# Three value blocks of the last pass turned ahead of wo's products: a decode step of two layers, forward and backward, on one core

## The chip, the core and the metric

The kernel runs on one core of a Trainium2 chip. The core has a matrix engine (TensorE: PE, with its weight loads PEld), a vector engine (VectorE: DVE), a scalar engine (ScalarE: ACT), a general engine (GpSimd: POOL), a queue engine (SyncE: SP) that here only issues transfers, and 16 DMA engines that move data between HBM and the on-chip memory SBUF. PE writes its results into PSUM, a small memory of eight banks, from where DVE or ACT fetch them. The metric is the device time of one execution in microseconds (us).

## The reference

Two attention layers and two MLP layers are interleaved and share their weights: A (attention with a key and a value cache of 16,384 positions, 2 sequences, 4 key/value heads, 32 query heads of 128), B (MLP), A, B. The kernel computes the output and the gradients of everything, the caches and the weights among them.

```python
def _A_ref(x, k_cache, v_cache, wq, wo):
    ...
    scores = jnp.einsum("bhqd,bhkd->bhqk", q, k) * (Dh ** -0.5)
    p = _softmax(scores, axis=-1)
    o = jnp.einsum("bhqk,bhkd->bhqd", p, v)
    return (lambda x, *d: x.transpose(*d))(o, 0, 2, 1, 3).reshape(B, Sq, Hq * Dh) @ wo
...
x = x + _A_ref(_layernorm(x, axis=-1), A_k_cache, A_v_cache, A_wq, A_wo)
x = x + _B_ref(_layernorm(x, axis=-1), B_w1, B_b1, B_w2, B_b2)
x = x + _A_ref(_layernorm(x, axis=-1), A_k_cache, A_v_cache, A_wq, A_wo)
x = x + _B_ref(_layernorm(x, axis=-1), B_w1, B_b1, B_w2, B_b2)
...
_out, _vjp = jax.vjp(_f, A_x, A_k_cache, A_v_cache, A_wq, A_wo, B_w1, B_b1, B_w2, B_b2)
_grads = _vjp(grad_out)
```

The last thing that the backward pass does is the attention backward of layer 0, the "last pass" here (`attn_bwd` with `l == 0`). For each of the 8 pairs of sequence and key/value head it needs the gradient's query vectors dO (the gradient that came down, times the transpose of wo), their products with all values V (the gradient of the probabilities), from these and the kept exponentials the gradient of the scores dS, and the products of dS with all keys (the gradient of the queries). In the same stretch the kernel writes the gradients of both caches (for both layers at once) and most weight gradients.

## The kernel before

**Passes.** The caches do not fit into SBUF, so every attention pass reads both from HBM once: forward layer 0, forward layer 1, backward layer 1, backward layer 0. A load brings 1 MB, 32 positions for each of the 128 partitions: a *chunk*, four *blocks* of 8 positions. Chunks go into slots (`slot0` to `slot15` and a few larger tiles that are free for a time).

**The order of the work.** All work is recorded first, as small functions with the slots that they use (`emit`), and replayed in that order (`Program.run`). The order on each engine is therefore the order of the recording; an engine that waits holds up everything behind it on the same engine. Loads are issued by SP in the order of their first use, each as early as a slot is free; SP's queue is in order too. A slot is free when the last recorded user of its chunk has run.

**A value block** (`kblock`). First a *turn* (L554): DVE transposes the block's 128x512 words in 32x32 squares into one of three `kT` buffers. Then a *use* (L567): eight PE products of the turned block with the spread query vectors `qbd`, into the PSUM bank `sc`. A use is recorded when two further turns have been recorded (`SKEW`), or at a step without a value block.

**The steps of the last pass.** `attn_bwd` runs steps 0 to 133. Step s turns value block s and multiplies key block s - 14 (L592); the last blocks are packed closer. In between stand the outputs: the dV and dK units (L1277, after a turn of the kept exponentials L1258 that ACT or DVE copies to `late`, L1265 or L1268), the weight gradients (L1337), and the spreading of q and dO over the partitions that these need (a transposition on PE L1225, a copy on ACT L1227 into `r16`, products L1235). Each output product fills a PSUM bank of 128x512; three banks take turns, and a cast by ACT (L276) or DVE (L279) empties each into a slot, from which POOL issues the store. Which of the two casts is fixed while recording, by a running account of both engines' load (`cast_out`, `copy_bf`, `load_of`).

**What stands ahead of step 0.** The gradient of layer 0's attention output is finished (L693, DVE: `gA_all`), wo's first 1024 rows, turned earlier, are multiplied with it (L470, 64 products, `here_products`), and `do_of` makes dO: L1018 and L1019 on DVE (`dof`, `qd`), four products L580 and two multiplications L583 that spread it into `qbd`, then the sums `dl` (L1022, a PE product L611, L1024). Three weight-gradient units of w2 (L1337) stand before L693 and one between wo's products; two more (`first[13:15]`) stand behind `do_of`. Then DVE clears an accumulator (L1057), and step 0 begins with the turn of value block 0. In step 4 `va` is spread (L511 on PE, L512 on DVE).

`wo_first` carries the recorded products of wo to `attn_bwd`; for layer 0 it is `(va0, wo_prods0)`. In these lines of step s the value blocks are recorded; `between` holds outputs and key blocks:

```python
for v in v_at.get(s, ()):
    pos, i = divmod(v, 16)
    if i % 4 == 0:
        kc[0] = ld_kv("V", order[pos], i // 4)
    kblock(kc[0], i, scb[0], order[pos], between)
```

Of the kernel before, what the change touches and what calls it, by code (L numbers as in the profile page):

```python
# [57 lines left out]
class Program:  # L58
# [12 lines left out]
    def emit(self, fn, uses=()):  # L71
        i = len(self.ops)
        self.ops.append((fn, tuple(uses)))
        for c in uses:
            if c.first is None:
                c.first = i
            c.last = i
# [105 lines left out]
def kernel(  # L183
# [25 lines left out]
    V = nc.vector  # L209
# [4 lines left out]
    B, _, D = A_x.shape  # L214
    _, HKV, SK, DH = A_k_cache.shape
# [14 lines left out]
    emit = P.emit  # L230
# [13 lines left out]
    scb = [[psp.tile([128, 8, 64], F32, name=f"sc{i}{f}") for f in range(2)] for i in range(2)]  # L244
# [37 lines left out]
    def dve(us):  # L282
        load_of("dve", us)
# [53 lines left out]
    def q_at(g):  # L337
        return 2 * (g % HKV % 2) + g // HKV
# [25 lines left out]
    saved = {}  # L364
# [11 lines left out]
    def ld_kv(nm, g, c):  # L376
        src = Kv if nm == "K" else Vv
        return P.chunk(lambda ap: nc.sync.dma_start(
            ap.rearrange("p (t d) -> p t d", d=128), src[g, :, c * 32:(c + 1) * 32, :]), (nm, g, c))
# [23 lines left out]
    pend = []  # L403
# [80 lines left out]
    def turned_products(ps, t, w0, nw, vb, first, last, parts=1):  # L484

        def f(k):
            def fn():
                tv = t.ap[:, 0:nw * 256].rearrange("p (w x e) -> p w x e", x=128, e=2)
                for w in range(k * nw // parts, (k + 1) * nw // parts):
                    for e in range(2):  # L490
                        J = (w0 + w) // 2
                        PE.matmul(ps(), lhsT=tv[:, w, :, e], rhs=vb()[:, 2 * (w % 2) + e, :, 2 * J:2 * J + 2],
                                  start=(first and w == 0 and e == 0), stop=(last and w == nw - 1 and e == 1),
                                  skip_group_check=True)
            return fn

        return [(f(k), [t]) for k in range(parts)]
# [47 lines left out]
            PE.matmul(ps[32 * a:32 * a + 32], lhsT=quadT[:], rhs=qa[:, :, a], start=True, stop=True)  # L545
        return ps.rearrange("p c (j b) -> p (c j) b", b=2)

    def kblock(c, i, bank, g, mids=()):

        hold = {}  # L550

        def turn():
            kT = ktp.tile([128, 1024], BF16, name="kT")
            V.transpose(out=kT[:].bitcast(I32).rearrange("p (w j m) -> p w j m", w=4, j=4),  # L554
                        in_=c.ap[:, (i % 4) * 1024:(i % 4 + 1) * 1024].bitcast(I32).rearrange(
                            "p (j w m) -> p w j m", w=4, j=4))
            dve(0.6)
            hold["kT"] = kT

        def use():  # L560
            kv = hold["kT"][:].rearrange("p (w m e) -> p w m e", w=4, e=2)
            sc = bank[i // 8].rearrange("p h (a y) -> p a h y", y=8)
            a0 = 4 * ((i // 4) % 2)
            for q in range(2):
                for w in range(2):
                    for e in range(2):
                        PE.matmul(sc[:, a0:a0 + 4, :, 2 * (i % 4) + q], lhsT=kv[:, 2 * q + w, :, e],  # L567
                                  rhs=qbd[:, q_at(g), 2 * w + e], start=(w == 0 and e == 0), stop=(w == 1 and e == 1))

        emit(turn, [c])  # L570
        for fn, us in mids:
            emit(fn, us)
        pend.append((use, ()))
        while len(pend) > SKEW:
            emit(*pend.pop(0))

# [413 lines left out]
    def wo_first_ops(l, k, ws=None):  # L990

        ws = ld_wo(k) if ws is None else ws
        ps = sb[0][:, 64:80].rearrange("p (r b) -> p r b", b=2)
        turns = [turn_here(ws[r // 4], (r % 4) * 1024, 8) for r in range(R)]
        prods = [here_products(ws[r // 4], (r % 4) * 1024, 8, lambda r=r: ps[:, r, :],
                               lambda o: gA_all[:, o, 2 * l:2 * l + 2]) for r in range(R)]
        return ws, turns, prods + [(lambda: do_of(l, k, ps), ())]
# [50 lines left out]
    def attn_bwd(l, order, gT, wo_first, outputs=None, mark=None, extra=None):  # L1048

        kvs = []  # L1050
        for g in order:
            if g % HKV not in kvs:
                kvs.append(g % HKV)
        vba, ops0 = wo_first
        for op in ops0:
            emit(*op)
        emit(lambda: V.memset(sb[0][:, 0:128], 0.0))  # L1057
        ev, wb = {}, {}
# [33 lines left out]
        for pos, g in enumerate(order):  # L1092
            quick = l == 0 and pos == G - 1
# [33 lines left out]
                for n, b in enumerate(ops):  # L1127
                    wb.setdefault((126 if l == 1 else 121) + n, []).append(b)

        kc, vc = {}, {}  # L1130
        n_steps = 128 + LAG_B if l == 1 else N_END
        k_at, v_at = {}, {}
        for v in range(128):
            quick = l == 0 and v >= 112
            k_at.setdefault(126 + v % 16 // 2 if quick else v + LAG_B, []).append(v)
            v_at.setdefault(112 + v % 16 // 2 if quick else v, []).append(v)
        s = 0
        while s <= n_steps:
            if s in (10, 74) and mark is not None:
# [3 lines left out]
            mids = []  # L1143
            for v in k_at.get(s, ()):
# [4 lines left out]
                c = vc[0]  # L1149
# [9 lines left out]
# [5 lines that stand above are left out]
                between = []  # L1164
# [130 lines left out]
    def y_rows(colT, j0, jn, q, at_):  # L1295

        def f():
            tp = ob().bitcast(BF16)[32 * q:32 * q + 4, 0:jn * 128].rearrange("p (a b) -> p a b", b=128)
            for j in range(jn):
                PE.transpose(tp[:, j, :], colT[:, j0 + j, :], ident[:])  # L1300
            S.copy(out=Y.ap[32 * q:32 * q + 4, at_:at_ + jn * 128], in_=flat(tp))
            load_of("act", 0.7)

        return f, [Y]
# [105 lines left out]
    up = [b * HKV + k for k in range(HKV) for b in range(2)]  # L1410
    down = up[::-1]
    marks = {}

    def mark(name):
        def f(n=0):
            marks[name, n] = len(P.ops)
        return f
# [61 lines left out]
    ws_o, wo_turns1, wo_prods = wo_first_ops(1, up[0] % HKV)  # L1479
# [28 lines left out]
    extra = {2: [(lambda: V.memset(fps1, 0.0), ())]}  # L1508
# [15 lines left out]
    for n, c in enumerate(ws1c):  # L1524
        t = w1t[n // 4][n % 4] if n == 7 else P.chunk()
        t1 += [] if n == 7 else turn_rows(c, t, 896)
        p1 += turned_products(lambda n=n: dm_0[:, n // 4], t, 14 * (n % 4), 14, vh0, n % 4 == 0, n % 4 == 3)
    attn_bwd(1, up, lambda: saved["g3"], (None, wo_prods), mark=mark("d1"), extra=extra)
    wo_prods0 = wo_first_ops(0, down[0] % HKV, saved["wo"])[2]


# [18 lines left out]
    first = [y_rows(gM_all, 0, 8, 0, 0)] + dw_units("h", 0, 0, pieces_rows(out_8, F, D))  # L1550
# [7 lines left out]
    va0, spread_a0 = spread(lambda: gA_all[:, :, 0:2], DJ, "va")  # L1558
# [3 lines left out]
    for u in first[9:12]:  # L1562
        emit(*u)
    emit(lambda: saved.__setitem__("g1", g1p[1]()))
    wo_prods0 = wo_prods0[:-1] + first[12:13] + wo_prods0[-1:] + first[13:15]
    extra = {4: [(spread_a0, ())]}

    sched = {}
# [20 lines left out]
    def outputs(s, rest=False):  # L1589
# [15 lines left out]
        state["credit"] = min(state["credit"], 2.0)  # L1605
        return res

    attn_bwd(0, down, lambda: saved["g1"], (va0, wo_prods0), outputs=outputs, extra=extra)
    slots = []
    for i, t in enumerate(slot_tiles):  # L1610
        until = marks[(HALF_AT + FULL_AT)[i], 0] if i < N_HALF + N_FULL else None
# [45 lines left out]
```

## Time and profile before

| what | value |
| --- | --- |
| three runs | 1099.14, 1101.32, 1103.54 us; median 1101.32 us |
| the profiled execution | 1099.65 us, of which 1097.9 us are the span from the first to the last instruction |
| moved by DMA in the span | 448.07 MB, mean 408 GB/s |
| busy in the span | PE 821.9 us (75%), DVE 753.4 (69%), ACT 487.8 (44%), POOL 176.2 (16%) |
| mean granted TensorE clock | 0.728 of full speed |
| turns of blocks (L554, DVE) | 436, 694 ns each on average |
| uses of blocks (L567, PE) | 4096 products, 128 weights x 32 columns |
| casts of outputs | by ACT (L276) 593 ns, by DVE (L279) 677 to 680 ns each |

All times of the profile come from one execution. Times of instructions count from the start of the span. "Idle before" is the time in which an engine stood still ahead of an instruction, with the instruction whose end released it. A matmul's length in the trace contains its latency, and matmuls overlap, so the cost of one in a row of many is the distance from start to start. The granted clock is the share of its full speed at which TensorE may run.

### The profile page before, as it was taken

To read this page: it belongs to the slowest core of one execution; us is meant where nothing else is said; L and a number is where in the kernel's file an instruction comes from. 1 tells how busy PE (TensorE), PEld (TensorE's weight loads), DVE (VectorE), ACT (ScalarE), POOL (GpSimd) and SP (SyncE) were. 2 spreads that over 40 slices of the span, in tenths; PEclk is the share of its full clock that TensorE was granted. 3 is DMA by queue.
4 is the path that set the end of the run, shared out by engine and by line. 5 is a ranking of instruction groups with operands and counts; after the bars stand their busy time and mean duration, and the time that the engine had idled before them with its cause. 6 is when DMAs were issued, how large, how long until landed. Compare 5 with 4: busy or idle time off the path is not lost. (4 is left out here: it accounts for less than half of the span.)

```text
span 1097.9 us, 34155 instructions
## 1 busy us (share of the span) xinstructions
PE 821.9 (75%) x14717; PEld 612.0 (56%) x14717; DVE 753.4 (69%) x1439; ACT 487.8 (44%) x1104; POOL 176.2 (16%) x550
## 2 busy tenths in 40 slices
PE   5665666457788657688868788988778888897885
PEld 4554555356777546587868675544444344443453
DVE  5864665168888727764746466977877778786874
ACT  0322222101242421234534436767666667676874
POOL 1000000001000000111211102332323333333330
PEclk9855555555555555558878667989998889898998
DMA  9999999999999999999999999999999999999996
GB/s 373 420 424 421 421 426 422 397 398 402 418 420 421 421 422 382 415 418 421 416 421 419 415 347 384 349 424 422 420 395 425 422 419 422 424 422 423 419 423 272
DMA packets 97404, 448.07 MB, mean 408 GB/s; under 512 B 7608, under 2 KB 11214, under 8 KB 58852
## 3 DMA queue, kind: packets, MB, share of 16 engines
q1 hardware_dynamic: 80004, 350.40, 78.5%
q0 software_dynamic: 17248, 95.48, 21.0%
q8 instruction: 115, 1.88, 0.6%
q14 instruction: 37, 0.30, 0.1%
HBM read 347.23 MB, written 98.62 MB: 406 GB/s over the span
## 5 line engine op out<-in xcount | busy, mean ns | idle before, releaser
L554 DVE STREAM_TRANSPOSE kT<-slot 128x512 int32<-128x512 int32 x436 | 293.3, 694 | 102.6 <-PE sc L567 89.3
L567 PE MATMUL sc<-qbd,kT 128*128 128x32 bf16 x4096 | 266.2, 224 | 12.8 <-DVE kT L554 10.5
L567 PEld LDWEIGHTS <-kT 128*128 128x128 bf16 x4096 | 211.4, 116 | 55.9 <-issue 25.3
L592 PEld LDWEIGHTS <-slot 128*128 128x128 bf16 x3488 | 143.9, 103 | 105.3 <-issue 56.3
L592 PE MATMUL sb<-xt,slot 128*128 128x8 bf16 x3488 | 160.7, 177 | 39.9 <-DMA slot<-in_A_v_cache_dram 21.5
L276 ACT CAST slot<-sc 128x512 bf16<-128x512 f32 x281 | 161.0, 593 | 59.5 <-PE sc L1337 29.3
L1277 PE MATMUL sc<-slot,late 128*128 128x512 bf16 x341 | 129.4, 402 | 28.3 <-DVE slot L279 8.1
L279 DVE CAST slot<-sc 128x512 bf16<-128x512 f32 x174 | 116.1, 677 | 26.7 <-PE sc L1277 11.3
L787 ACT ACTIVATE e<-sc 128x512 bf16<-128x512 f32 x32 | 19.0, 597 | 235.5 <-DVE sc L784 169.2
L276 ACT CAST slot<-sb 128x512 bf16<-128x512 f32 x148 | 87.8, 593 | 39.8 <-PE sb L1337 19.1
L460 ACT COPY slot<-tp 128x512 int32<-128x512 int32 x84 | 48.9, 585 | 105.5 <-PE tp L457 90.7
L1277 PE MATMUL sb<-slot,late 128*128 128x512 bf16 x171 | 69.2, 405 | 14.4 <-ACT slot L276 5.9
L1277 PEld LDWEIGHTS <-late 128*128 128x128 bf16 x512 | 44.7, 99 | 61.7 <-issue 49.2
L602 ACT COPY xt<-e 32x128 int32<-32x128 int32 x256 | 75.6, 295 | 3.9
L457 PE MATMUL tp<-ident,slot 128*128 128x128 bf16 x736 | 71.6, 260 | 2.7 <-DMA slot<-in_A_wq_dram 1.7
L1337 PE MATMUL sc<-slot,late 128*128 128x512 bf16 x169 | 66.5, 415 | 7.9 <-DVE slot L279 5.3
L279 DVE CAST slot<-sb 128x512 bf16<-128x512 f32 x81 | 55.0, 680 | 19.5 <-PE sb L1277 10.7
L457 PEld LDWEIGHTS <-slot 128*128 128x128 bf16 x736 | 57.4, 119 | 4.2 <-DMA slot<-in_A_wq_dram 1.8
L602 POOL COPY xt<-ds 32x64 int32<-32x64 int32 x128 | 29.5, 230 | 184.8 <-DVE ds L1070 125.2
L662 POOL TENSOR_TENSOR m_rstd<-ln_vpe,neghalf 128x2 f32<-128x2 f32 x2 | 1.4, 718 | 349.6 <-DVE ln_vpe L660 349.6
L602 POOL COPY xt<-late 32x64 int32<-32x64 int32 x240 | 55.1, 230 | 14.4 <-DVE late L1070 2.0
L442 DVE STREAM_TRANSPOSE slot<-slot 128x1024 int32<-128x1024 int32 (+1 forms) x46 | 52.9, 1177 | 1.0 <-PE sb L470 0.5
(300 smaller groups left out, 1081.9 us busy)
## 6 DMA issues: line engine op xcount, KB each, us to landing
slot<-in_A_k_cache_dram SPq DMA_DIRECT2D x104, 1024.0 KB, 15.8
slot<-in_A_v_cache_dram SPq DMA_DIRECT2D x101, 1024.0 KB, 17.1
out_dram<-slot POOLq DMA_DIRECT2D x55, 1024.0 KB, 15.7
slot<-in_A_wq_dram SPq DMA_DIRECT2D x25, 1024.0 KB, 17.4
slot<-in_A_wo_dram SPq DMA_DIRECT2D x25, 1024.0 KB, 19.1
out_dram<-slot POOLq DMA_DIRECT2D x40, 512.0 KB, 15.8
slot<-in_B_w_dram SPq DMA_DIRECT2D x22, 896.0 KB, 15.5
slot<-in_B_w_dram SPq DMA_DIRECT2D x11, 1024.0 KB, 13.6
```

The costliest lines, as they stand in the source:

```text
L276: S.copy(out=dst, in_=src)
L279: V.tensor_copy(out=dst, in_=src)
L442: V.transpose(out=t.ap[:, h * nw * 256:(h + 1) * nw * 256].bitcast(I32).rearrange("p (w j m) -> p w j m", j=4, m=32), in_=c.ap[:, 0:4 * nc ...
L457: PE.transpose(tp[:, j * 128:(j + 1) * 128], c.ap[:, off + j * 128:off + (j + 1) * 128], ident[:])
L460: S.copy(out=d.bitcast(I32), in_=tp.bitcast(I32))
L554: V.transpose(out=kT[:].bitcast(I32).rearrange("p (w j m) -> p w j m", w=4, j=4), in_=c.ap[:, (i % 4) * 1024:(i % 4 + 1) * 1024].bitcast(I ...
L567: PE.matmul(sc[:, a0:a0 + 4, :, 2 * (i % 4) + q], lhsT=kv[:, 2 * q + w, :, e], rhs=qbd[:, q_at(g), 2 * w + e], start=(w == 0 and e == 0), ...
L592: PE.matmul(acc, lhsT=c.ap[:, n * 128:(n + 1) * 128], rhs=xv[:, i // 4, t // 2, :, 2 * (i % 4) + t % 2], start=(fresh and i == 0 and t == ...
L602: (GP.tensor_copy if on[t % len(on)] == "g" else S.copy)(out=d[32 * t:32 * t + 32, c0:c0 + cn, j, :], in_=s[32 * j:32 * j + 32, c0:c0 + cn ...
L787: S.activation(out=e_of(l, g)[:, 8 * f:8 * f + 8].rearrange("p a h b -> p h a b"), in_=sc[f][:].rearrange("p h (a b) -> p h a b", b=8), fu ...
L1277: PE.matmul(ps, lhsT=hold["blk"][:, j, :], rhs=flat(qm(w)[:, hf * 4:hf * 4 + 4, :]), start=True, stop=True)
L1337: PE.matmul(ps, lhsT=hold[j // 4 * 4][:, j % 4, :], rhs=Y.ap[:, y_at + c0:y_at + c0 + cn], start=True, stop=True)
```

## The change

For the last pass alone, the turns of value blocks 0, 1 and 2 are recorded ahead of wo's 64 products (L470), and their uses right behind `do_of`, ahead of the two weight-gradient units `first[13:15]`, which are passed on separately for that (`ops1`). Block 3 is turned in step 0, so that steps 1 to 3 hold no value block; blocks 4 and on stay where they were. Since step 1 has no block, the use of block 3 is recorded there. The helper `kblock` is split, so that a block's turn and use can be recorded apart. Nothing is computed that was not computed before.

```diff
-    def kblock(c, i, bank, g, mids=()):
+    def kblock_parts(c, i, bank, g):
...
-        emit(turn, [c])
+        return (turn, [c]), (use, ())
+
+    def kblock(c, i, bank, g, mids=()):
+
+        turn, use = kblock_parts(c, i, bank, g)
+        emit(*turn)
         for fn, us in mids:
             emit(fn, us)
-        pend.append((use, ()))
+        pend.append(use)
         while len(pend) > SKEW:
             emit(*pend.pop(0))
...
-        vba, ops0 = wo_first
-        for op in ops0:
+        vba, ops0, ops1 = wo_first
+        kc, vc = {}, {}
+        ahead = []
+        if l == 0:
+            kc[0] = ld_kv("V", order[0], 0)
+            ahead = [kblock_parts(kc[0], i, scb[0], order[0]) for i in range(3)]
+        for op in [turn for turn, _ in ahead] + ops0 + [use for _, use in ahead] + ops1:
             emit(*op)
         emit(lambda: V.memset(sb[0][:, 0:128], 0.0))
...
-        kc, vc = {}, {}
         n_steps = 128 + LAG_B if l == 1 else N_END
         k_at, v_at = {}, {}
         for v in range(128):
             quick = l == 0 and v >= 112
             k_at.setdefault(126 + v % 16 // 2 if quick else v + LAG_B, []).append(v)
-            v_at.setdefault(112 + v % 16 // 2 if quick else v, []).append(v)
+            if v >= len(ahead):
+                v_at.setdefault(112 + v % 16 // 2 if quick else 0 if v == len(ahead) else v, []).append(v)
...
-    attn_bwd(1, up, lambda: saved["g3"], (None, wo_prods), mark=mark("d1"), extra=extra)
+    attn_bwd(1, up, lambda: saved["g3"], (None, wo_prods, []), mark=mark("d1"), extra=extra)
...
-    wo_prods0 = wo_prods0[:-1] + first[12:13] + wo_prods0[-1:] + first[13:15]
+    wo_prods0 = wo_prods0[:-1] + first[12:13] + wo_prods0[-1:]
...
-    attn_bwd(0, down, lambda: saved["g1"], (va0, wo_prods0), outputs=outputs, extra=extra)
+    attn_bwd(0, down, lambda: saved["g1"], (va0, wo_prods0, first[13:15]), outputs=outputs, extra=extra)
```

In the built program every engine has as many instructions as before, and the sequences of SP and POOL are the same, with the same slots. On DVE three turns (L554) stand between L693 and L1018; on PE their 24 products (L567) stand behind L611, and those of block 3 between the first four and the second four products of L1235. A few casts and copies change sides between ACT and DVE.

## The prediction

> **What bounds the kernel now.** I read the forty slices of the page first. DMA stands at 9 nearly throughout, so the kernel is paced by its 448 MB wherever the transfers are fed. The slices of interest are the 24th to 26th (631 to 713 us), where the rate falls to 347, 384 and 349 GB/s while its neighbours hold 415 to 424: that is where the last pass begins.
>
> ```profile
> PEclk9855555555555555558878667989998889898998
> DMA  9999999999999999999999999999999999999996
> GB/s 373 420 424 421 421 426 422 397 398 402 418 420 421 421 422 382 415 418 421 416 421 419 415 347 384 349 424 422 420 395 425 422 419 422 424 422 423 419 423 272
> ```
>
> Second view: busy time of each engine in stretches of 5 us (columns: PE, PEld, DVE, ACT, POOL, granted clock, DMA share, GB/s).
>
> ```profile
> 665.00:670.00 5.00, 3.48 (x27) 2.02 (x26) 2.84 (x9) 2.56 (x6) 0.72 (x1) 0.50 1.00 420
> 670.00:675.00 5.00, 5.00 (x53) 2.94 (x50) 3.06 (x5) 3.67 (x8) 0.00 (x0) 0.61 1.05 420
> 675.00:680.00 5.00, 4.56 (x58) 2.44 (x57) 3.47 (x6) 4.51 (x11) 0.57 (x1) 1.00 1.02 426
> 680.00:685.00 5.00, 4.03 (x51) 2.27 (x50) 4.50 (x9) 4.18 (x10) 2.76 (x11) 1.00 0.76 287
> 685.00:690.00 5.00, 4.64 (x57) 2.42 (x56) 4.20 (x9) 3.58 (x7) 1.94 (x8) 1.00 0.75 256
> 690.00:695.00 5.00, 4.75 (x59) 2.84 (x58) 4.63 (x9) 4.03 (x8) 1.31 (x3) 1.00 0.91 294
> 695.00:700.00 5.00, 4.68 (x43) 2.01 (x40) 4.66 (x9) 4.18 (x9) 0.24 (x1) 1.00 0.99 341
> ```
>
> The reader is to see three stages. To 675 us PE works at half clock with DVE and ACT half idle, and DMA is full. From 680 to 700 DMA starves: against 422 GB/s it loses 5 us x (4 - (287 + 256 + 294 + 341)/422) = 6.0 us, while DVE is busy 4.2 to 4.7 us of 5. From 700 on (424 in 700 to 705) it is fed again. So the last pass ends earlier or later by what the engines' arrival in 680 to 700 gains or loses, since the transfers that are missing there wait for freed slots.
>
> Third view: SyncE's queue in order of time, which shows that these loads are gated by value blocks. The load at 682.78 follows a DVE turn (L554) after 10.8 us of waiting, the one at 691.55 another after 8.3 us.
>
> ```profile
> 671.62 0.33 SPq L378 DMA_DIRECT2D slot<-in_A_k_cache_dram  x1
> 682.78 0.38 SPq L383 DMA_DIRECT2D slot<-in_A_wo_dram  x1
> 691.55 0.33 SPq L378 DMA_DIRECT2D slot<-in_A_v_cache_dram  x1
> ```
>
> Fourth view: the instructions in order of time where the change is (start, length, instruction; in brackets the idle time before it and what ended it).
>
> ```profile
> 662.29 0.16 DVE L693 TENSOR_TENSOR gM<-lb_u,sc 128x16 f32<-128x16 f32 x1
> 664.77 0.17 DVE L1018 TENSOR_TENSOR dof<-sb,rbc 128x16 f32<-128x16 f32 x1 [2.32 <-PE sb L470]
> 667.20 1.86 DVE L554 STREAM_TRANSPOSE kT<-slot 128x512 int32<-128x512 int32 x3
> 667.67 0.38 PE L1225 MATMUL sc<-ident,qd 128*16 128x128 bf16 x2
> 668.72 0.58 PE L1235 MATMUL sb<-r,sel 16*128 16x128 bf16 x4 [0.66 <-ACT r L1227]
> 669.66 0.64 PE L1258 MATMUL tp<-ident,e 128*64 128x128 bf16 x8
> 670.23 1.04 PE L567 MATMUL sc<-qbd,kT 128*128 128x32 bf16 x16
> 670.34 0.37 ACT L1265 COPY late<-tp 128x256 int32<-128x256 int32 x1
> 670.88 1.31 DVE L554 STREAM_TRANSPOSE kT<-slot 128x512 int32<-128x512 int32 x2 [1.81 <-PE sc L567]
> 671.08 0.62 PE L1277 MATMUL sc<-slot,late 128*128 128x512 bf16 x1
> 676.53 0.69 DVE L279 CAST slot<-sb 128x512 bf16<-128x512 f32 x1 [1.58 <-PE sb L1337]
> ```
>
> Between 667 and 676.5 DVE waits for PE four times (1.81, 0.56, 0.46 and 1.58 us), PE only once for longer than 0.2 us (0.66). So PE's order sets the pace here, and from 676.5 on DVE does.
>
> **The change, part by part.** In the built program the same instructions stand on every engine, and SP's and POOL's sequences are those of before. What moves: three turns on DVE, 24 products of three blocks and 8 of the fourth on PE, and some casts between ACT and DVE.
>
> *The three turns* (1.86 us by their row) go into DVE's idle 2.32 us ahead of L1018: the last instruction before it ends at 662.29 + 0.16 = 662.45, the turns would end at 664.31, 0.46 before L1018 is due. They need the first value chunk, whose load was issued at 645.4; with the page's median of 17.1 us to landing it is there at 662.5. Price 0; with the longest landing the page gives for loads (19.1 us) they would start at 664.5 and hold L1018, and all that follows it, until 666.4: +1.6 as the upper bound. They take all three kT buffers, which nothing else asks for until block 3.
>
> *The 24 products* come behind L611, where PE is free at 666.73, ahead of L1337's two, L1225, and so ahead of ACT's r16 copy (L1227) and the first L1235. Their price by the row of 16 (670.23 to the next product's start at 671.08: 0.85 us, 53 ns each) is 24 x 53 ns = 1.28 us, on PE's path, because L1225 waits for nothing but its turn. The eight of block 3 go in between the two groups of L1235: +0.43. Taken away ahead of the first L1277 are 16: -0.85. So PE's own work in front of L1277 grows by 0.86 us.
>
> *A cover that goes.* The 16 products at 670.23 hid ACT's copy of the turned block (L1265, over at 670.71): L1277 needs it. Now nothing stands between L1258 and L1277. L1258 starts at 669.66 + 1.28 + 0.43 = 671.37; copy and hand-over took 670.71 - 669.66 = 1.05 us; L1277 starts at about 672.46 instead of 671.08: +1.38. That is 0.86 of work and 0.52 of cover lost.
>
> *What comes back.* The products of blocks 2 and 3 no longer stand between the output products that follow (0.45 us at 671.91, 0.32 at 673.72). But these are paced by ACT's casts, which start 0.48 us apart: from 671.73 to 675.98 there are eight steps, 4.25 us, of which 8 x 0.48 = 3.84 would be left. So 0.4 comes back, 0.77 at most if PE alone counted. The bounds of the whole are +0.6 and +1.4, and I take +1.0, as ACT's row is without gaps.
>
> *The late end.* DVE's cast at 676.53 waits for PE and slides by the same 1.0; behind it DVE queues the turns whose ends release the loads at 682.78 and 691.55. Its idle time in 680 to 700 is 20 - (4.50 + 4.20 + 4.63 + 4.66) = 2.0 us, in bits of a few tenths that are waits for PE's output products, so I let it give nothing back; if it all did, the price is 0. The key load at 671.62 goes out some 3.6 us earlier (its slot is free behind block 3's turn in step 0, about 668), but DMA is full at 420 GB/s there, so that buys nothing.
>
> Sum: 0 + 1.38 - 0.4 = +1.0 us. The profiled execution took 1099.65 us, its span 1097.9 and 1.75 around it: 1100.65. The median shown is 1101.32, 1.67 above the profiled one, so I forecast 1102.3.
>
> A rule of the Trainium skill speaks about the half clock: "TensorE: Matmul & The Clock Gate", section "Part 1: The HAM clock gate", says that the clock is throttled by default and is released only after a busy window of some 3.4 us. The trace agrees as far as it goes: 0.50 to 670, 0.61 in the next 5 us, in which PE is busy 5.00 of 5, then 1.00. By that rule the idle hole that the change puts in front of L1277 may keep the clock down for another window; the third rival prices this from rows.
>
> **The rivals.**
>
> *Faster: DVE paces the pass.* Then 1.86 us of turns have left a busy stage, and the 1.81 us idle at 670.88 (a wait for a kT buffer) goes with them: 1101.32 - 1.8 = 1099.5. For it: DVE is the busiest engine in 680 to 700. Against it: in 671 to 676.5 DVE waits for PE and not the other way round. If earlier turns also fed the whole starved stretch, its 6.0 us would go: 1095.3. That needs every slot of the stretch freed in time; the turns behind 682.78 and 691.55 are blocks 11 and 15, whose places do not move.
>
> *No effect.* The 2.0 us of DVE idle swallow the delay: 1101.3. For it: the stages share their casts between two engines. Against: DVE's gaps there are themselves waits for PE.
>
> *Slower: the clock stays at half.* The place is PE from 673.9 on. The price: an output product starts 0.40 us after the one before at half clock (671.08 to 671.48), 0.21 at full (677.28 to 677.49), so the 4.56 us of PE work in 675 to 680 would take 8.7; a stretch at half clock loses 1 - 5/8.7 = 0.43 of itself. The trace's clock at 725 to 735 (0.51 and 0.81) shows one half stretch of 4.9 + 1.9 = 6.8 us: it would cost 2.9 us, in all 1105.2. It passes 0.5% from about 10 us of half clock on (4.5/0.43). For it: the hole in front of L1277 falls into the stretch (670 to 675) in which PE was busy 5.00 of 5 and after which the clock rose. Against: 24 products now fill 1.3 us in 666 to 668 without a gap, which could as well bring the clock up earlier.
>
> **How the numbers follow.** Forecast (+0.3 to +2) 0.40; slower by the clock 0.27, a good half of it beyond 0.5%; faster 0.20, of which the starved stretch largely closed 0.13; no effect 0.13. Half a per cent, 5.5 us, is about what a measurement of this kernel tells from no change (the three runs span 4.4 us). With a little for their scatter: faster by over 0.5% (below 1095.8) 0.15, within 0.65, slower (above 1106.8) 0.20. The range goes from the closed stretch, 1095.3, to two half-clock stretches on top of the forecast, 1102.3 + 2 x 2.9: 1095.3 to 1108.1. The forecast's own range is 1100.5 to 1104.
>
> **What would show it.** Right: three turns between 662.4 and 664.8, L1018 still at about 664.8; 24 products in some 1.3 us behind L611; L1235 at about 670.0, L1277 at about 672.5 after an idle hole of half a us; the loads at 682.78 and 691.55 about 1 us later; the GB/s of 680 to 700 no better. Wrong: L1277 no later than 671.1, the load at 682.78 earlier, over 300 GB/s in 685 to 690, or a clock that turns at another time than 673.9.

## The result, and the profile after

| | before | after |
| --- | --- | --- |
| median of 22 runs each | 1101.24 us (1099.14 to 1104.58) | 1104.29 us (1101.69 to 1108.64) |
| ratio after/before, 95% interval | | 1.0029 [1.0020, 1.0038] |
| profiled execution | 1099.65 us, span 1097.9 | 1102.53 us, span 1100.8 |
| 680 to 700 us of the profile | 295 GB/s | 242 GB/s |

The changed kernel is 3.05 us slower by the medians (1104.29 - 1101.24), 0.29% by the ratio: no change by the bound of half a per cent, yet clearly not nothing, since the interval excludes 1. On another chip (run e8 below) the ratio was 1.0016 [1.0007, 1.0025]. In the changed kernel's profile the lines of `attn_bwd` that were named so far have numbers that are 5 or 10 higher (L583 is L588, L611 is L616, L592 is L597, L1018 is L1023; L1225 is L1235, L1235 is L1245, L1258 is L1268, L1265 is L1275, L1277 is L1287, L1337 is L1347); L276, L279, L470, L511 and L554 to L567 stay.

The forty slices of the changed kernel:

```profile
PEclk9999999997555555568868666989988899898998
DMA  9999999999999999999999998999999999999996
GB/s 371 420 423 420 421 426 422 400 386 400 419 421 421 422 421 384 416 416 420 417 421 418 415 365 353 347 421 422 419 382 424 423 420 421 426 421 422 419 423 275
```

In the stretch of interest, the 24th to 26th slices, the rates are 365, 353 and 347 GB/s, where they were 347, 384 and 349: 15 less in sum over some 82 us. These slices also hold a stretch ahead of the change, 630 to 660 us, in which this execution moved more (366 GB/s against 350); the loss behind it is larger, as the next view shows. Most other slices agree within a few GB/s. The clock line differs over the first third of the kernel too, and there the GB/s are the same.

Busy time of each engine in stretches of the changed kernel (PE, PEld, DVE, ACT, POOL, granted clock, DMA share, GB/s):

```profile
670.00:675.00 5.00, 4.38 (x30) 1.89 (x28) 1.64 (x3) 3.62 (x8) 0.06 (x1) 0.50 1.03 415
675.00:680.00 5.00, 5.00 (x39) 2.51 (x39) 2.12 (x4) 3.23 (x8) 0.57 (x1) 0.53 0.95 393
680.00:685.00 5.00, 4.71 (x68) 2.66 (x66) 4.77 (x9) 4.77 (x11) 1.01 (x4) 1.00 0.31 129
685.00:690.00 5.00, 3.41 (x34) 1.62 (x32) 4.53 (x8) 3.21 (x7) 3.21 (x14) 1.00 0.98 334
690.00:695.00 5.00, 4.85 (x74) 3.00 (x73) 4.08 (x7) 3.68 (x8) 1.36 (x3) 1.00 0.65 264
695.00:700.00 5.00, 4.77 (x42) 2.21 (x40) 4.62 (x9) 4.40 (x9) 0.44 (x1) 1.00 0.95 242
```

Two things are to be seen. The stretch 675 to 680 was at full clock before and is at 0.53 now. And 680 to 700 starves more: against 422 GB/s it now loses 20 x (1 - 242/422) = 8.5 us, where it lost 20 x (1 - 295/422) = 6.0. The 2.5 us between them are most of the 2.9 us by which the span grew (1100.8 - 1097.9).

The loads that were to come about 1 us late, in SyncE's queue (before: 671.62, 682.78, 691.55):

```profile
667.42 0.33 SPq L378 DMA_DIRECT2D slot<-in_A_k_cache_dram  x1
684.96 0.38 SPq L383 DMA_DIRECT2D slot<-in_A_wo_dram  x1
693.79 0.33 SPq L378 DMA_DIRECT2D slot<-in_A_v_cache_dram  x1
```

The key load went out early, as forecast, 3.32 us behind L1023 rather than 6.84. The two that starve DMA are 2.2 us later on the clock of the span. Since two executions don't reach the last pass at the same moment (the first instruction of `do_of` started at 664.77 before and at 664.10 after), all later comparisons count from that instruction. Counted so, the first of them is 684.96 - 664.10 = 20.86 us away, where it was 682.78 - 664.77 = 18.01: 2.85 us late.

The instructions in order of time, where the change is:

```profile
661.62 0.16 DVE L698 TENSOR_TENSOR gM<-lb_u,sc 128x16 f32<-128x16 f32 x1
661.70 1.89 DVE L554 STREAM_TRANSPOSE kT<-slot 128x512 int32<-128x512 int32 x3
664.10 0.17 DVE L1023 TENSOR_TENSOR dof<-sb,rbc 128x16 f32<-128x16 f32 x1 [0.51 <-PE sb L470]
...
666.06 1.44 PE L567 MATMUL sc<-qbd,kT 128*128 128x32 bf16 x24
667.31 0.61 PE L1347 MATMUL sb<-slot,late 128*128 128x512 bf16 x1
...
669.33 0.58 PE L1245 MATMUL sb<-r,sel 16*128 16x128 bf16 x4 [0.67 <-ACT r L1237]
669.84 0.61 PE L567 MATMUL sc<-qbd,kT 128*128 128x32 bf16 x8
670.38 0.60 PE L1245 MATMUL sc<-r,sel 16*128 16x128 bf16 x4
670.92 0.64 PE L1268 MATMUL tp<-ident,e 128*64 128x128 bf16 x8
...
672.02 0.61 PE L1287 MATMUL sc<-slot,late 128*128 128x512 bf16 x1 [0.47 <-ACT late L1275]
```

The reader is to see each step of the sum in its place: three turns in DVE's idle time, of which 0.51 of 2.32 us is left and whose releaser is still PE's L470; 24 products in 1.25 us (666.06 to 667.31); the wait for ACT's copy `r16`, as long as before (0.67), after them rather than filled by them; eight more products between the two groups of L1245; and in front of the first output product (L1287) a hole of 0.47 us that ends with ACT's copy.

### The profile page after: what moved, and what is told of

It is laid out like the page before. It is cut to its first block, busy times and chain, and to the rows that moved or that the text cites. A ratio compares the mean times of both kernels' runs of the same rounds, so it can differ in the third digit from the quotient of the medians.

```text
span 1100.8 us, 34151 instructions
## 1 busy us (share of the span) xinstructions
PE 819.6 (74%) x14717; PEld 608.3 (55%) x14717; DVE 755.7 (69%) x1439; ACT 487.4 (44%) x1104; POOL 176.3 (16%) x550
## 5 line engine op out<-in xcount | busy, mean ns | idle before, releaser
L554 DVE STREAM_TRANSPOSE kT<-slot 128x512 int32<-128x512 int32 x436 | 293.9, 695 | 101.3 <-PE sc L567 85.9
L567 PE MATMUL sc<-qbd,kT 128*128 128x32 bf16 x4096 | 264.8, 223 | 12.4 <-DVE kT L554 11.4
L567 PEld LDWEIGHTS <-kT 128*128 128x128 bf16 x4096 | 210.5, 116 | 50.2 <-issue 18.0
L597 PEld LDWEIGHTS <-slot 128*128 128x128 bf16 x3488 | 143.1, 103 | 109.8 <-issue 58.5
L597 PE MATMUL sb<-xt,slot 128*128 128x8 bf16 x3488 | 159.6, 176 | 43.5 <-DMA slot<-in_A_v_cache_dram 24.4
L276 ACT CAST slot<-sc 128x512 bf16<-128x512 f32 x284 | 161.8, 592 | 59.5 <-PE sc L1287 25.1
L1287 PE MATMUL sc<-slot,late 128*128 128x512 bf16 x341 | 128.9, 401 | 30.6 <-DVE slot L279 10.7
L279 DVE CAST slot<-sc 128x512 bf16<-128x512 f32 x171 | 114.9, 679 | 26.8 <-PE sc L1287 8.4
L276 ACT CAST slot<-sb 128x512 bf16<-128x512 f32 x145 | 85.7, 591 | 39.2 <-PE sb L1347 16.3
L1287 PE MATMUL sb<-slot,late 128*128 128x512 bf16 x171 | 69.0, 403 | 17.0 <-DVE slot L279 7.1
L1287 PEld LDWEIGHTS <-late 128*128 128x128 bf16 x512 | 44.7, 99 | 62.4 <-issue 49.6
L279 DVE CAST slot<-sb 128x512 bf16<-128x512 f32 x84 | 57.3, 682 | 20.7 <-PE sb L1347 7.5
L457 PE MATMUL tp<-ident,slot 128*128 128x128 bf16 x736 | 69.2, 253 | 2.0 <-DMA slot<-in_A_wq_dram 1.7
L1347 PE MATMUL sc<-slot,late 128*128 128x512 bf16 x169 | 66.2, 415 | 5.1 <-DVE slot L279 2.5
L457 PEld LDWEIGHTS <-slot 128*128 128x128 bf16 x736 | 55.2, 116 | 3.6 <-DMA slot<-in_A_wq_dram 1.8
```

Source lines behind the costliest of these rows:

```text
L276: S.copy(out=dst, in_=src)
L279: V.tensor_copy(out=dst, in_=src)
L457: PE.transpose(tp[:, j * 128:(j + 1) * 128], c.ap[:, off + j * 128:off + (j + 1) * 128], ident[:])
L597: PE.matmul(acc, lhsT=c.ap[:, n * 128:(n + 1) * 128], rhs=xv[:, i // 4, t // 2, :, 2 * (i % 4) + t % 2], start=(fresh and i == 0 and t == ...
L1287: PE.matmul(ps, lhsT=hold["blk"][:, j, :], rhs=flat(qm(w)[:, hf * 4:hf * 4 + 4, :]), start=True, stop=True)
L1347: PE.matmul(ps, lhsT=hold[j // 4 * 4][:, j % 4, :], rhs=Y.ap[:, y_at + c0:y_at + c0 + cn], start=True, stop=True)
```

## The experiments

All of them were profiled, and nearly all timed. The table holds, behind the start of `do_of` (L1018 of before) in each kernel's own profile: the first output product, the rise of the granted clock, and the first of the two late loads. The moment of the rise is worked out from stretches of 3 us, since the traces hold no other values of the clock than 0.5 and 1: a mean of 0.88 in 679 to 682 means half clock for (1 - 0.88)/0.5 x 3 = 0.72 us, so the changed kernel's clock rose at 679.72, 15.62 behind 664.10. The ratio is to the runs of the kernel before on the same chip.

| kernel | first output product | clock rises | late load | ratio to before |
| --- | --- | --- | --- | --- |
| before | 6.31 | 9.1 | 18.0 | |
| after, profiled with the result | 7.92 | 15.6 | 20.9 | 1.0029 [1.0020, 1.0038] |
| e8 after, again | 7.92 | 13.1 | 20.0 | 1.0016 [1.0007, 1.0025] |
| e1 turns only | 6.31 | 10.8 | 18.4 | 1.0001 [0.9990, 1.0011] |
| e2 after, holes filled with repeats | 8.23 | 12.5 | 20.2 | 1.0019 [1.0008, 1.0029] |
| e3 before, waits filled | 6.31 | 9.1 | 18.0 | 1.0003 [0.9992, 1.0014] |
| e4 before, cover moved | 7.08 | 10.5 | 18.9 | 1.0013 [1.0003, 1.0024] |
| e5 uses inside the waits | 6.30 | 11.2 | 18.6 | 1.0005 [0.9995, 1.0016] |
| e6 before, 24 products ahead of L1225 | about 8.1 | 5.8 | 19.3 | 1.0017 [1.0005, 1.0029] |
| e7 after, block 3 as cover | 7.28 | 17.7 | 20.9 | 1.0010 [1.0001, 1.0020] |
| e9 after, repeats between outputs | 7.92 | 13.5 | 20.5 | 1.0013 [1.0005, 1.0022] |
| e10 before, none between outputs | about 7.3 | 9.9 | 18.9 | 1.0000 [0.9991, 1.0010] |
| e11 as e9, one run | 7.92 | 12.7 | 20.2 | |
| e12 as e10, one run | about 7.3 | 9.6 | 18.9 | |

("About": the trace lacks the record of that product, and the time is put back from the next one.) The kernels of e3, e4, e6, e10 and e12 are the one before with the edit shown, the others the changed one.

### Which part is it: turns, cover, or clock?

Four runs on one chip. **e1** keeps the early turns, and with them the new distribution of casts between ACT and DVE, and puts the uses back to where they were:

```diff
-        for op in [turn for turn, _ in ahead] + ops0 + [use for _, use in ahead] + ops1:
+        for op in [turn for turn, _ in ahead] + ops0 + ops1:
...
-            if v >= len(ahead):
-                v_at.setdefault(112 + v % 16 // 2 if quick else 0 if v == len(ahead) else v, []).append(v)
+            v_at.setdefault(112 + v % 16 // 2 if quick else v, []).append(v)
...
+                if v < len(ahead):
+                    for fn, us in between:
+                        emit(fn, us)
+                    pend.append(ahead[v][1])
+                    while len(pend) > SKEW:
+                        emit(*pend.pop(0))
+                    between = []
+                    continue
```

> Three turns ahead of wo's products as in the changed kernel, PE's order as in the kernel before (uses of blocks 0 to 3 where they stood, block 3 turned in step 3). The casts stand on ACT and DVE as in the changed kernel. Path theory (the delay is PE's work and the lost cover ahead of the first output product) and clock theory (the clock rises later because PE's dense stretch is broken): the first L1277 about 6.3 us behind L1018's start as before, the clock turns 8 to 10 us behind L1018, ratio to before 1.000 (+-0.0008). Theory of the casts that changed sides between ACT and DVE: ratio 1.002 to 1.003, as the changed kernel.

Measured: 1101.49 against 1101.35 us, 1.0001. The first output product is where it was before (6.31). So neither the early turns nor the casts that changed sides are the loss, and they are no gain either; it is the uses (with block 3's place, which e1 puts back too).

**e2** is the changed kernel with the use of block 3 repeated, so that PE has products where the change left it waiting:

```diff
+            if l == 0 and s == 0:
+                again = pend[0]
+            if l == 0 and s in (2, 3, 4, 5):
+                emit(*again)
```

> The changed kernel with 32 more products: block 3's use is repeated (it writes the same numbers again) at the four places where the kernel before has the uses of blocks 0 to 3, so that PE's order from L1258 on is dense again. Path theory: 16 products of 53 ns in a hole of 0.47 us delay the first L1277 by 0.4 us more, ratio to before about 1.003, no better than the changed kernel's 1.0029. Clock theory: the clock turns 8 to 10 us behind L1018 instead of 15.6, which gives back about 2 us: ratio 1.001 to 1.0015, faster than the changed kernel with more work. Casts theory: 1.003.

Measured: 1103.85 us, 1.0019, with the clock rising at 12.5 us, earlier than in either profile of the changed kernel (15.6, 13.1), but later than before (9.1). PE has no wait from 670.13 us on (the first L1249, which is L1235 of before), and the rise is 7.2 us later, at 677.35. A filled hole doesn't bring the old clock back.

**e3** is the kernel before with 16 products that nobody reads (`filler`, identity by identity into an unused part of a bank) in three waits of PE: 5 behind L545, 6 behind L580, 5 behind L1225.

```diff
+    def filler(n):
+        for _ in range(n):
+            PE.matmul(sb[0][:, 384:512], lhsT=ident[:], rhs=ident[:], start=True, stop=True, skip_group_check=True)
...
+            if parts:
+                filler(5)
...
+            if l == 0 and not filled:
+                filled.append(1)
+                filler(6)
...
+            if pos == 0:
+                filler(5)
```

> The kernel before with 16 idle products of 128 columns (identity by identity, into PSUM columns that nobody reads) in three of PE's waits: 5 behind L545, 6 behind L580, 5 behind L1225, 0.5 to 0.65 us each, inside waits of 0.66 to 0.82 us. Path theory: nothing moves, ratio 1.000 (+-0.0008). Clock theory: PE has no idle time from 662.8 us on, the clock turns one to two stretches of 3.4 us earlier than at 673.9, PE's work until then takes half the time: 1.4 to 3 us less, ratio 0.9973 to 0.9987.

Measured: 1.0003, and the rise at 9.1 us, as before. The stretches of e3 (same columns as above):

```profile
664.00:667.00 3.00, 2.80 (x60) 2.06 (x58) 0.92 (x5) 0.92 (x2) 0.73 (x1) 0.50 1.04 431
667.00:670.00 3.00, 2.63 (x18) 1.75 (x19) 2.11 (x5) 1.44 (x4) 0.72 (x1) 0.50 1.00 419
670.00:673.00 3.00, 3.00 (x40) 2.08 (x38) 1.31 (x2) 1.98 (x5) 0.00 (x0) 0.50 1.02 402
673.00:676.00 3.00, 2.88 (x24) 1.20 (x21) 1.75 (x3) 2.69 (x6) 0.00 (x0) 0.77 1.06 431
```

PE is busy 2.80 of 3 and 2.63 of 3 us (2.15 and 2.34 before), and the clock waits for the same moment. More work in front of the stretch is not what raises it.

**e4** is the kernel before with the 16 products that covered ACT's copy recorded earlier, ahead of the second group of L1235, and nothing else:

```diff
+                if l == 0 and v == 2:
+                    between = [pend.pop(0), pend.pop(0)] + between
                 kblock(kc[0], i, scb[0], order[pos], between)
```

> The kernel before with the 16 products of blocks 0 and 1 ahead of the second four products of L1235 instead of behind L1258: the same work ahead of the first L1277, but ACT's copy (L1265) is uncovered, a hole of some 0.5 us on PE. Path theory: +0.5 us, ratio 1.0005. Clock theory: the hole falls into the stretch that had let the clock rise at 673.9, it rises some 3 to 7 us later: 1.5 to 3 us more, ratio 1.002 to 1.003. Casts theory: 1.000.

Measured: 1103.29 against 1101.35 us, 1.0013 [1.0003, 1.0024]. In its order of time (L1260, L1267 and L1279 are L1258, L1265 and L1277 of before):

```profile
669.40 1.04 PE L567 MATMUL sc<-qbd,kT 128*128 128x32 bf16 x16
...
670.91 0.64 PE L1260 MATMUL tp<-ident,e 128*64 128x128 bf16 x8
672.02 0.61 PE L1279 MATMUL sc<-slot,late 128*128 128x512 bf16 x1 [0.47 <-ACT late L1267]
```

The same hole of 0.47 us as in the changed kernel, from the moved cover alone, with the same instructions on PE. The first output product comes 7.08 - 6.31 = 0.77 us later, the load 18.94 - 18.01 = 0.93. So the lost cover is real, and it reaches the end. But the clock rises at 10.5 us here, hole and all, so the hole isn't what holds the clock in the changed kernel either.

### Is it time on PE's path, and can the change be mended?

Four runs on another chip, **e8**, the changed kernel again, among them.

> The changed kernel once more, for a second profile. If its order holds the clock down, the clock turns again some 15 us behind L1018 and the load behind block 11 comes at +20.5 to +21. If the 15.6 us of the first profile was the chance of where the clock's windows of 3.4 us lay, it turns at 10.5 to 13 us and the load comes at +19.3 to +20. Ratio to before 1.002 to 1.0038 either way.

Its first output product is at 7.92 us, to the hundredth where the first profile had it, but its clock rose 2.5 us sooner, as its stretches show:

```profile
673.00:676.00 3.00, 2.85 (x13) 0.93 (x11) 1.64 (x3) 2.79 (x6) 0.00 (x0) 0.50 1.02 418
676.00:679.00 3.00, 3.00 (x35) 1.42 (x34) 1.18 (x3) 2.23 (x5) 0.57 (x1) 0.74 0.97 408
```

The rise is at 676 + (1 - 0.74)/0.5 x 3 = 677.56, 13.11 behind its 664.45, and its load is 20.86 - 20.04 = 0.82 us less late. Both are nearer to what was expected if the first profile's 15.6 us was chance. The program is the same in these two, so the pair gives an estimate of the clock's price: 0.82/2.51 = 0.33 us of delay for each us of half clock. Two more pairs with one order of PE give 0.42/1.70 = 0.25 (before and e1) and 0.36/0.84 = 0.43 (e9 and e11). The prediction had 0.43.

**e6** puts 24 unread products in front of L1225 (here L1231) of the kernel before: a plain delay in the place of the moved uses, and no cover moved. They take 672.88 - 670.18 = 2.70 us.

```diff
         def rows16():
+            if pos == 0:
+                filler(24)
```

> The kernel before with 24 idle products of 128 columns (into PSUM columns that nobody reads) ahead of L1225: 24 x 0.107 = 2.57 us of PE work on the path, with no hole and no cover moved. Path theory (a delay here reaches the end undiminished, since the loads of 680 to 700 wait for value blocks): first L1277 at +8.9 us behind L1018, the load behind block 11 at +20.0 to +20.6, ratio to before 1.0018 to 1.0024. Theory that the stretch swallows delays of this size and the changed kernel's loss is all the late clock: ratio 1.000 to 1.001.

Measured: 1103.44 against 1101.64 us, 1.0017 [1.0005, 1.0029]. Its order of time:

```profile
670.18 2.77 PE L1215 MATMUL sb<-ident 128*128 128x128 bf16 x24 [0.22 <-DVE sb L1057]
672.88 0.38 PE L1231 MATMUL sc<-ident,qd 128*16 128x128 bf16 x2
```

Its stretches:

```profile
668.00:671.00 3.00, 1.96 (x15) 1.56 (x15) 1.98 (x7) 1.45 (x3) 0.00 (x0) 0.50 0.98 415
671.00:674.00 3.00, 2.55 (x27) 2.16 (x25) 0.71 (x2) 0.43 (x2) 0.72 (x1) 0.64 1.02 412
674.00:677.00 3.00, 2.30 (x44) 1.62 (x43) 1.75 (x4) 2.40 (x5) 0.00 (x0) 1.00 1.06 428
```

This is the only kernel whose clock rose early, at 673.16 us, 0.3 us behind the last of the 24, or 5.75 behind L1018 rather than 9.1. Even so the load is 19.26 - 18.01 = 1.25 us late and the kernel 1.9 us [0.5, 3.2] slower. Time put in front of L1225 is lost even with the clock on its side.

**e7** is the changed kernel with block 3's use behind L1268 (L1258 of before), where it covers the copy:

```diff
-            if s not in v_at and pend:
+            if s not in v_at and pend and not (l == 0 and s == 1):
```

> The changed kernel with block 3's use behind L1258, as cover of ACT's copy, instead of between the two groups of L1235. Path theory: the first L1277 starts 0.4 us earlier than in the changed kernel, 7.5 us behind L1018, ratio to before 1.002 to 1.0025 (changed kernel: 1.0029). Theory that the hole holds the clock down: no hole, so the clock turns 10 to 12 us behind L1018 and the load of block 11 comes at 19 to 19.5: ratio 1.001 to 1.0015.

Its order of time:

```profile
671.26 0.64 PE L1268 MATMUL tp<-ident,e 128*64 128x128 bf16 x8
671.83 0.61 PE L567 MATMUL sc<-qbd,kT 128*128 128x32 bf16 x8
672.37 0.61 PE L1287 MATMUL sc<-slot,late 128*128 128x512 bf16 x1
```

The hole is gone, and the first output product comes 7.92 - 7.28 = 0.64 us earlier than in the changed kernel. Yet the kernel gained nothing over e8 that can be told (1.0010 [1.0001, 1.0020] and 1.0016 [1.0007, 1.0025]), and in its profile the clock rose later than in any other, as its stretches show:

```profile
676.00:679.00 3.00, 3.00 (x25) 1.37 (x23) 0.78 (x2) 1.79 (x4) 0.57 (x1) 0.50 1.01 421
679.00:682.00 3.00, 3.00 (x26) 1.83 (x25) 2.39 (x5) 2.02 (x4) 0.00 (x0) 0.50 1.01 421
682.00:685.00 3.00, 3.00 (x42) 1.74 (x42) 2.82 (x5) 2.30 (x6) 0.00 (x0) 0.86 0.18 76
```

PE is without a wait from 673.65 on, and the rise is at 682.84, some 9.2 us later.

**e5** looks for a version that is better than both. It is e1 with the first use behind L1225, where PE waits for the `r16` copy anyway, and the next two behind L1258 as cover. Block 3 is turned as soon as the first use frees its buffer, and the key load goes out 4.60 us behind `do_of`'s start rather than 6.84.

```diff
+                    if v == 0:
+                        emit(*ahead[0][1])
+                    elif v == 2:
+                        emit(*ahead[1][1])
+                        emit(*ahead[2][1])
```

> Three turns ahead of wo's products; block 0's use in PE's wait behind L1225 (0.43 us of work in a wait of 0.66), blocks 1 and 2 as cover of ACT's copy behind L1258, block 3 turned and used as in the kernel before. Path theory: the first L1277 6.3 us behind L1018 as before, and the eight products between the second and third output product are gone (0.45 us): the load that waits for block 11's turn 17.5 to 18.0 us behind L1018 (before: 18.0), ratio to before 0.9993 to 1.000. Theory that early uses cost by themselves (clock, or PSUM and kT buffers): the load at 19 or later, ratio 1.001 and above.

Measured: 1101.23 against 1101.64 us by the medians, a ratio of 1.0005 [0.9995, 1.0016]: no gain. PE has its first output product at 6.30 us with one use more already done and the key load is 2.2 us sooner, yet the late load comes at 18.6 instead of 18.0, with a clock that rose at 11.2: between the two expectations, and no gain from either. No version beat the kernel before.

### Why does the clock rise late?

e4, e7 and e3 had ruled out the hole and the amount of work ahead. What was left is the order further on: in the kernel before, products of value blocks stand between the first output products, in the changed one none do. **e9** and **e11** (the same kernel) put such products there in the changed kernel (the edit of e2 with `s in (4, 5)`), **e10** and **e12** take them away in the kernel before:

```diff
+                while l == 0 and v == 3 and pend:
+                    emit(*pend.pop(0))
```

> The changed kernel with 16 more products: block 3's use repeated (same numbers) at the two places between output products where the kernel before has the uses of blocks 2 and 3; the hole in front of the first L1277 stays. New clock theory (not the hole: the products between the output products keep PE full while ACT's casts pace it, and let the clock rise): first L1277 at +7.9 us behind L1018 as in the changed kernel, the clock turns 2.8 to 5 us behind it, at 10.7 to 12.9; the load behind block 11 at +19.3 to +20. Chance theory (the clock's windows lie where they happen to): 13 to 17 us, load at 20 to 20.9. Ratio to before 1.001 to 1.002 against 1.0015 to 1.0029.

> The kernel before with the uses of blocks 2 and 3 ahead of the first output product, behind those of 0 and 1: cover kept, no hole, no turn moved, but no products between the output products that follow. First L1277 at +7.1 us behind L1018 (16 x 53 ns later than 6.3). New clock theory: the clock turns 5 us or more behind it, at +12.3 or later; load behind block 11 at +19.3 or later; ratio to before 1.0012 to 1.0025. Chance theory: the clock turns at 9 to 12, load at +18.7 to +19.2, ratio 1.0005 to 1.001.

> The kernel with the use of block 3 repeated between the output products once more, for a second profile of its clock: new clock theory 10.7 to 12.9 us behind L1018, chance theory 13 to 17.

> The kernel with no products between the output products once more, for a second profile of its clock: new clock theory at +12.3 us behind L1018 or later, chance theory 9 to 12.

The stretches of e10, in which all 32 products stand behind L1258 and none between the outputs:

```profile
670.00:673.00 3.00, 2.78 (x42) 2.35 (x43) 1.31 (x2) 1.00 (x3) 0.00 (x0) 0.50 1.03 409
673.00:676.00 3.00, 2.66 (x14) 1.06 (x13) 1.64 (x3) 2.81 (x6) 0.00 (x0) 0.68 1.05 427
```

(The trace lacks the record of the first output product, so that the first row has some 0.2 us less of PE than there was.) Its clock rose at 674.92, 9.86 behind L1018, and at 9.62 in e12: early without products between. In e9 and e11 it rose at 13.5 and 12.7: late with them. So this theory fell as well. e10 also delays the first output product, by about 1 us, and its load by 0.86; its ratio, 1.0000 [0.9991, 1.0010], beside e4's 1.0013 at the same delay shows where timed runs stop to tell: a delay of 0.9 us is at their limit.

What the thirteen other profiles show together (all but e6) is a division by order. The seven in which no product of a value block stands ahead of L1225 (before, e1, e3, e4, e5, e10, e12) have the rise at 9.1 to 11.2 us; the six with the 24 products behind L611 (after, e8, e2, e7, e9, e11) at 12.5 to 17.7. The two groups, which were formed after the runs, don't overlap.

The clock records of the traces make this firmer. In each of the fourteen profiles all changes of the clock lie on a raster of 3.413 us (before: half clock from 639.76 to 673.90 us, ten steps of it), and from one execution to the next the raster mostly lies differently against the pass. So the clock rose only at a step of the raster, and where the raster lies can by itself shift a rise by up to one step. Profiles whose rasters lie within 0.8 us of each other can be compared step by step. Before and e3 rose at 9.12 and 9.10 us behind `do_of`, e2 and e11 at 12.45 and 12.68, one step later, the changed kernel at 15.62, two steps later, and e6 at 5.75, one step sooner. e10 and e12 rose at 9.86 and 9.61, e8 and e9 at 13.11 and 13.52, one step later; e1, e4 and e5 at 10.82, 10.50 and 11.24, e7 at 17.73, two steps later. That the order with the moved uses makes the clock rise one or two steps later is shown; by what, is not.

## Why the prediction was right, and where it was not

The forecast was 1102.3 us, +1.0, no change by half a per cent. Measured are +3.05 us on one chip and, by e8's ratio, 0.0016 x 1101.64 = +1.8 [0.8, 2.8] on another. Sign and class were right, and so was PE's path up to the first output product; the median of 1104.29 lies 0.3 above the forecast's own range (1100.5 to 1104) and inside the whole one. That it lies inside is owed to the width of the range: 1104.29 is nearer to the 1105.2 of the third rival, which had a chance of 0.27, than to 1102.3. One of the prediction's own signs of being wrong came true, a clock that turns at another time than 673.9, and the two loads were 2.85 us late rather than about 1 (2.03 in e8, for the first).

**The three turns at price 0: right.** They ran from 661.70 to 663.59 in DVE's idle time, L1023 was still released by PE's L470, and e1 measured them alone at 1.0001. The rival that DVE paces the pass fell with the same run.

**The products: right in number and place.** The 24 took 1.25 us (1.28 forecast), and the first L1245 came 5.23 us behind L1023 instead of 3.95, 1.28 later. Block 3's eight were mis-sized a little: with them the eight products of L1245 took 670.92 - 669.33 = 1.59 us instead of 0.94, so 0.65 and not 0.43.

**The lost cover: right.** The hole is 0.47 us long and ends with ACT's copy; e4 makes it alone and e7 takes it away alone. The first output product came 7.92 - 6.31 = 1.61 us later, 1.38 forecast; block 3's 0.22 is the difference. (The forecast's own terms, 671.37 + 1.05, give 672.42 and not 672.46; the step from the turn to the product measured 672.02 - 670.92 = 1.10.)

**What comes back: mis-sized; the late end: open.** From the first output product on, the next seven steps between ACT's casts took 676.34 - 672.67 = 3.67 us, where they took 675.50 - 671.73 = 3.77: 0.10 came back there, not 0.4. What the 1.5 us that are left became at the late load can only be estimated. By the clock's price of 0.33 the two profiles of the changed kernel leave 2.85 - 0.33 x 6.5 = 0.7 and 2.03 - 0.33 x 4.0 = 0.7 us for the path; with 0.25 and 0.43 as the price it is 0.1 to 1.2. The 1.0 of the forecast lies within. e4 and e10 agree with that (0.93 - 0.33 x 1.4 = 0.5, and 0.86 - 0.33 x 0.8 = 0.6, of a first output product 0.8 and 1.0 us late). Others don't: by the same price e7 leaves nothing of 1.0 us (2.9 - 0.33 x 8.6 = 0.1), e2 1.1 of 1.9 (2.2 - 0.33 x 3.4), and e6, whose clock was 3.4 us early, all of its delay and more (1.25 + 0.33 x 3.4 = 2.4, of some 1.8). So one price for all places does not hold, and the division between path and clock is not firm. Nor is it shown where a part of the path's delay went: DVE's idle time in 680 to 700, from which the sum let nothing come back, is 2.0 us before and after (20 - 4.77 - 4.53 - 4.08 - 4.62).

**The clock: the step that was mis-sized.** The forecast's sum took the clock's rise as unchanged, a term of nothing, and left a late clock to the third rival, which put 6.8 us of half clock on top of the path (1102.3 + 2.9 = 1105.2). That way is what came: a rise 6.5 us later in the profile with the result, 4.0 later in e8, at 0.33 us each 2.1 and 1.3 us of late load. With the path's 0.7 this makes the 2.85 and 2.03 measured, but the 0.7 is what was left of them, so the sum is no test of it. The starved stretch handed most of the delay to the end (2.5 of 2.9 us). The rival's length of 6.8 us and its price of 0.43 were near what came (4.0 to 6.5, and 0.25 to 0.43); that the forecast held nothing of it, not even weighted by its chance of 0.27, is where the forecast went wrong. The rule of the Trainium skill that stood beside this rival, in "TensorE: Matmul & The Clock Gate", section "Part 1: The HAM clock gate" (one busy window of about 3.4 us releases the clock), does not settle it. The traces agree for e4, where the clock rose at 675.44, 3.42 us behind the hole's end at 672.02. They do not for e7, where 9.2 us without a wait were needed, nor for e2, where PE had no wait from 670.13 on and the step of the raster from 670.52 to 673.93 was not followed by the rise, which came a step later. In e10 the step that ended with the rise, 671.51 to 674.92, holds a wait of 0.15 us (at 673.64). And the reason that the prediction gave for a late clock, the hole, is not the cause (e4, e7).

**The early key load buys nothing: right.** It went out 3.5 us sooner, and e5, which has it 2.2 us sooner without the delay, has 1.0005.

What stays open: what of the changed order keeps the clock down. One order alone scatters by up to 2.5 us (13.1 and 15.6 in the changed kernel), so with one profile for most kernels only the division of the two groups, and the steps between profiles with a like raster, are firm. That the path keeps 0.7 us is worked out with a price from three pairs, not measured at one clock, and the other kernels do not bear it out.

## What to carry to other kernels

Work that is to fill an engine's wait must be recorded inside that wait: the 24 products went in front of the chain that ends in it, so that the wait for `r16` stayed (0.67 us) and the chain behind it slid by 1.28 us. Even work inside the wait (e5) brought nothing here that the timed runs can tell. Before instructions are moved away, look at what they hid where they stood: an edit that only takes a cover away (e4) made the first output product 0.77 us and the late load 0.93 us later. And where a stage at half clock feeds one that starves DMA, a shift of the clock's rise is to be added to the shift of the path, here at an estimated 0.25 to 0.43 us for each us.

## What the runs showed of the hardware beyond that

- The clock was at half for most of the first 460 us in the profile of before, and at full for the first 250 us or so in that of after (the first nine digits of its clock line). The rate of the second to seventh slice is the same, 420 to 426 GB/s in both: where DMA sets this kernel's pace, the clock cost nothing that the rate shows, and the mean granted clock (0.728 before, 0.824 after, and after is the slower) is no measure of this kernel's time.
- 24 products without a pause (e6) were followed by the rise 3.0 us after their start (673.16 - 670.18), while PE at 2.80 and 2.63 of 3 us with small waits (e3) didn't bring it forward by a step of the raster.
